# One unit of a decode-attention kernel loads half its keys and values in a row order that uses eight DMA engines

## The chip, the core and the metric

The kernel runs on one core of a Trainium2 chip. The metric is device time in microseconds (us) of one execution. All timed runs below are of the fast state (the one look named *alone* has no known state), and every ratio uses runs of the kernel before from the same chip and the same rounds. The kernel before takes 453.46 us (median; 453.44 to 454.08 in four runs).

Names: PE is the tensor engine, DVE and ACT the vector and scalar engines, SP the engine that issues the loads here. A *DMA engine* is one of the core's 16 transfer engines; it has nothing to do with PE, DVE and the rest. A *packet* is one record of the trace's DMA rows; here one row of keys or values for one SBUF partition, mostly 8 or 16 KB (4096 packets of 8 KB and 8064 of 16 KB in the load queue of the kernel before). A *landing* is one increment of a transfer's semaphore. A plain load has 16 landings in the trace, which I read as one for each DMA engine, and it is complete at the last one: PE started on unit 24's keys at 285.69 us, and their 16th landing was at 285.64 us.

## The reference

Two decode attentions with one query token each, concatenated. A sees all 8192 keys, B only the last 2048. There are 4 batches, 32 query heads, 8 key heads of width 128, all in bf16:

```python
q = (x @ wq)                         # 4 x 1 x 512 times 512 x 4096
scores = einsum("bhqd,bhkd->bhqk", q, k) * Dh ** -0.5   # k: cache, 8 heads, repeated 4 times
p = softmax(scores)
o = einsum("bhqk,bhkd->bhqd", p, v)
return o.reshape(B, 1, 4096) @ wo
```

There is little arithmetic per byte: 184.6 MB are read, mostly the two caches.

## The kernel before

The work is cut into 40 units: 8 of B (units 0 to 7), then 32 of A, one for each pair of key head and batch. A unit of A has 2 MB of keys and 2 MB of values. Partition p gets 64 consecutive keys (16 KB), so a load is 128 rows of 16 KB:

```python
NKS, NVS, NKT, NPT = 3, 4, 4, 3                # buffers for K, V, ...
def kv_src(cache, u, q=None):
    un = units[u]
    if un["P"] == 0:                           # attention A
        ap = cache[un["b"], un["g0"]].rearrange("(p t) d -> p t d", p=128)
        return ap if q is None else ap[:, q * TQ:(q + 1) * TQ, :]
    ...                                        # attention B: two halves
def sp_K(u):                                   # issue of a unit's keys, on SP
    waits = [("T", tjob_idx[(u - NKS, NB - 1)])] if u >= NKS else []
    ...
    op("sp", dma(kv_dst(K_sb, u % NKS, u), kv_src(KC[units[u]["P"]], u)), waits=waits, inc=("K", u))
```

PE transposes the keys (`L309` below), multiplies them with the queries (`L340`), and later multiplies the probabilities with the values (`L366`). It starts on a unit when the whole K load has landed. SP issues the K load of unit u when PE has transposed unit u-3, and the V load when PE has used the values of unit u-4. The order of keys within a unit does not matter to softmax, as long as K and V use the same one.

## Time and profile before

| | before |
|---|---|
| time, median | 453.46 us |
| share of the time in which the 16 DMA engines were busy with the load queue | 97.1% |
| rate in the middle of the run | 423 to 429 GB/s |
| PE busy | 83% |
| a 16 KB packet (trace, median of 274 to 294 us) | 613 ns |

The page of the kernel before: the span, the DMA rows in 40 slices, the queues, and the chain of waits that ended last.

```profile
span 452.2 us, 14586 instructions
...
DMA  8999999999999999999999999999999999999972
GB/s 346 401 414 418 451 402 418 419 417 428 408 416 430 424 423 424 428 426 424 428 425 425 428 423 429 423 425 423 425 426 426 427 425 423 430 420 428 423 332 80
DMA packets 17189, 185.51 MB, mean 410 GB/s; under 512 B 1748, under 2 KB 2280, under 8 KB 4712
...
q1 hardware_dynamic: 17048, 184.56, 97.1%
q8 instruction: 53, 0.87, 0.8%
...
DMA 60%; PE 33%; issue 3%; DVE 2%; ACT 1%; POOL 0%; POOLq 0%
```

Loads bound the kernel: the rate is flat near 425 GB/s from the first tenth to the end, and the chain is 60% DMA. PE's own lines (name, count, then busy us and ns of one, then the idle time before them and who ended it) show that it waits for keys and values:

```profile
L309 PE MATMUL ps<-identf,K_sb 128*128 128x128 f32 x1280 | 225.0, 337 | 37.7 <-DMA K_sb<-in_A_k_cache_dram 25.8
L366 PE MATMUL ps<-PT,V_sb 128*128 128x4 bf16 (+1 forms) x2560 | 76.6, 165 | 9.7 <-DMA V_sb<-in_A_v_cache_dram 7.5
```

The landings of the last load (last quarter of unit 39's values), read from the trace's semaphore records as us after the first one, show something that no share of busy time shows. It is not a view of the page, so it stands in an ordinary fence:

```
before   first 435.62 us: 0.0 0.2 0.4 0.8 0.8 1.8 2.3 4.7 | 9.3 9.4 9.4 9.7 10.7 10.8 10.9 11.0   last 446.62 us
```

Eight engines are done some 9 us (on average) before the other eight. The late ones lost their time in steps of some 1.5 us, near the packets of the instruction queue (q8 above: 53 packets of 16 KB and about 1.07 us each). That these packets are what makes the eight late is a reading of the trace.

### The profile page before, as it was taken

The page shows a single profiled execution, that of the slowest core. Times are in us where ns is not written, and L with a number is a line of the kernel's source. Part 1 is how long each engine was busy: PE and PEld are TensorE (multiplying, and loading weights), DVE is VectorE, ACT ScalarE, POOL GpSimd, SP SyncE. Part 2 cuts the span into 40 slices and gives each one's busy share as a digit, 9 for nine tenths or more (in the row PEclk, how much of TensorE's full clock was granted, in tenths as well). Part 3 has the DMA queues.
Part 4 walks back from the last instruction along what each step waited for, and adds up shares of the span by engine and source line. Part 5 has one row for each costly group of instructions (what it writes and reads, how often), then busy time and mean ns, then how long its engine had stood idle before and what let it go on. Part 6 is the DMA issues. An engine that isn't in the chain of part 4 may idle for free.

```text
span 452.2 us, 14586 instructions
## 1 busy us (share of the span) xinstructions
PE 374.6 (83%) x6781; PEld 344.9 (76%) x6781; DVE 196.4 (43%) x451; ACT 178.1 (39%) x202; POOL 35.6 (8%) x93
## 2 busy tenths in 40 slices
PE   0682379999859998989978898878989899888996
PEld 0682279987858797989768888867979799788895
DVE  0351225745634453434434543444445435434362
ACT  1150214524433362534334453434444434434261
POOL 1100000100100110000100010001000000000010
PEclk9996655859887985968878896969768858888596
DMA  8999999999999999999999999999999999999972
GB/s 346 401 414 418 451 402 418 419 417 428 408 416 430 424 423 424 428 426 424 428 425 425 428 423 429 423 425 423 425 426 426 427 425 423 430 420 428 423 332 80
DMA packets 17189, 185.51 MB, mean 410 GB/s; under 512 B 1748, under 2 KB 2280, under 8 KB 4712
## 3 DMA queue, kind: packets, MB, share of 16 engines
q1 hardware_dynamic: 17048, 184.56, 97.1%
q8 instruction: 53, 0.87, 0.8%
q14 instruction: 8, 0.07, 0.0%
q10 hardware_dynamic: 16, 0.01, 0.0%
q0 software_dynamic: 64, 0.01, 0.0%
HBM read 184.56 MB, written 0.01 MB: 408 GB/s over the span
## 4 chain that ended last, share of the span: by engine, by line
DMA 60%; PE 33%; issue 3%; DVE 2%; ACT 1%; POOL 0%; POOLq 0%
DMA K_sb<-in_A_k_cache_dram 30%; DMA V_sb<-in_A_v_cache_dram 24%; PE ps L309 18%; DMA W<-in_A_wq_dram 6%; PE ps L366 6%; PE ps L340 4%; PE ps L452 2%; PE ps L255 2%; DVE KT_sb L317 1%; ACT KT_sb L318 1%; DVE M L470 1%; PE ps L442 0%; DVE Dt L508 0%; PE ps L406 0%; DVE xo_sb L567 0%
## 5 line engine op out<-in xcount | busy, mean ns | idle before, releaser
L318 ACT ACTIVATE KT_sb<-ps 128x1024 bf16<-128x1024 bf16 x160 | 163.5, 1022 | 250.4 <-PE ps L309 250.2
L309 PE MATMUL ps<-identf,K_sb 128*128 128x128 f32 x1280 | 225.0, 337 | 37.7 <-DMA K_sb<-in_A_k_cache_dram 25.8
L309 PEld LDWEIGHTS ps<-identf,K_sb 128*128 128x128 f32 x1280 | 184.4, 174 | 50.8 <-DMA K_sb<-in_A_k_cache_dram 28.9
L317 DVE COPY KT_sb<-ps 128x512 int32<-128x512 int32 x160 | 110.4, 690 | 148.6 <-PE ps L309 147.9
L366 PE MATMUL ps<-PT,V_sb 128*128 128x4 bf16 (+1 forms) x2560 | 76.6, 165 | 9.7 <-DMA V_sb<-in_A_v_cache_dram 7.5
L366 PEld LDWEIGHTS ps<-PT,V_sb 128*128 128x128 bf16 x2560 | 71.0, 97 | 10.7 <-DMA V_sb<-in_A_v_cache_dram 8.3
L340 PEld LDWEIGHTS ps<-RQA,KT_sb 128*128 128x128 bf16 x2048 | 71.6, 99 | 3.6 <-issue 0.6
L340 PE MATMUL ps<-RQA,KT_sb 128*128 128x8 bf16 x2048 | 72.6, 167 | 0.9 <-ACT KT_sb L318 0.4
L540 POOL PARTITION_ALL_REDUCE LB<-L x40 | 17.3, 432 | 154.9 <-DVE L L531 154.9
L479 POOL PARTITION_ALL_REDUCE MB<-M x32 | 11.9, 371 | 176.9 <-DVE M L470 176.9
L470 DVE TENSOR_REDUCE M<-ps 128x4 f32<-128x256 f32 (+1 forms) x40 | 19.1, 477 | 12.7 <-PE ps L340 12.7
L557 DVE TENSOR_TENSOR OTg<-ps,RL 128x4 bf16<-128x4 f32 (+1 forms) x40 | 6.9, 174 | 40.2 <-PE ps L366 40.2
L531 DVE TENSOR_REDUCE L<-PT 128x4 f32<-128x256 bf16 (+1 forms) x40 | 21.9, 546 | 2.6 <-ACT PT L519 2.1
L340 PEld LDWEIGHTS ps<-RQB,KT_sb 128*128 128x128 bf16 x512 | 18.7, 102 | 2.6 <-issue 0.9
L340 PE MATMUL ps<-RQB,KT_sb 128*128 128x16 bf16 x512 | 19.0, 173 | 1.4 <-issue 0.9
L519 ACT ACTIVATE PT<-Dt 128x256 bf16<-128x256 f32 (+1 forms) x40 | 18.1, 452 | 3.3 <-DVE Dt L508 3.2
L452 PE MATMUL ps<-W,OL 128*4 128x512 bf16 x60 | 17.1, 432 | 0.0
L255 PE MATMUL ps<-xT,W 128*128 128x4 bf16 x256 | 7.5, 166 | 11.0 <-DMA W<-in_A_wq_dram 10.6
L255 PEld LDWEIGHTS ps<-xT,W 128*128 128x128 bf16 x256 | 7.2, 104 | 11.1 <-DMA W<-in_A_wq_dram 10.7
L508 DVE TENSOR_TENSOR Dt<-ps,MB 128x256 f32<-128x256 f32 x32 | 13.3, 415 | 0.5 <-POOL MB L479 0.5
L234 PE MATMUL ps<-ident,xo_sb 4*128 4x4 bf16 x8 | 0.6, 170 | 14.2 <-POOL identf L581 14.2
L414 DVE CAST OL<-ps 32x16 bf16<-32x16 f32 (+1 forms) x36 | 6.5, 182 | 11.1 <-PE ps L406 10.7
(43 smaller groups left out, 53.5 us busy)
## 6 DMA issues: line engine op xcount, KB each, us to landing
K_sb<-in_A_k_cache_dram SPq DMA_DIRECT2D x32, 2048.0 KB, 22.1
V_sb<-in_A_v_cache_dram SPq DMA_DIRECT2D x31, 2048.0 KB, 27.0
K_sb<-in_B_k_cache_dram SPq DMA_DIRECT2D x16, 1024.0 KB, 18.7
V_sb<-in_B_v_cache_dram SPq DMA_DIRECT2D x16, 1024.0 KB, 21.8
W<-in_B_wq_dram SPq DMA_DIRECT2D x1, 4096.0 KB, 12.6
W<-in_B_wo_dram SPq DMA_DIRECT2D x1, 4096.0 KB, 34.3
W<-in_A_wq_dram SPq DMA_DIRECT2D x1, 4096.0 KB, 29.2
W<-in_A_wo_dram SPq DMA_DIRECT2D x1, 3584.0 KB, 30.1
```

What stands on the lines that cost most here:

```text
L255: ins = pe.matmul(out=bk[:, hl * Bn:(hl + 1) * Bn], lhsT=W1wq[:, c, hq * DH:(hq + 1) * DH], rhs=xT[:, P, c, :], start=(c == 0), stop=(c == ...
L309: ins = pe.transpose(out=bkf[:, pi * 128:(pi + 1) * 128], in_=K_sbf[:, slot, t0:t0 + 2, :].rearrange("p t d -> p (t d)"), identity=identf[ ...
L317: return e.tensor_copy(out=KT_sb.bitcast(I32)[:, tj % NKT, :], in_=bkf.bitcast(I32)[:, :])
L318: return e.activation(out=KT_sb[:, tj % NKT, :], in_=bk[:, :], func=ACTF.Copy)
L340: ins = pe.matmul(out=stb[:, t * CPT:(t + 2) * CPT], lhsT=ktv[:, pi, :, e], rhs=rhs, start=(e == 0), stop=(e == 1))
L366: ins = pe.matmul(out=otb[:, s * CPT:(s + 1) * CPT], lhsT=V_sb[:, vs, t, :], rhs=pt_cols(u, t * CPT, CPT), start=(j == 0), stop=(j == J - 1))
L452: ins = pe.matmul(out=opb[0:Bn, 0:D], lhsT=lhsT, rhs=wo_view[:, hq0 // REP + i // REP, i % REP, :], start=(first and i == 0), stop=(last a ...
L470: return dve.tensor_reduce(out=M1[:, 0:NC].rearrange("p (s h) -> p s h", h=CPT), in_=stb[:, 0:NT * CPT].rearrange("p (s j h) -> p s h j", ...
L508: return dve.tensor_tensor(out=Dt[:, 0:NT * CPT].rearrange("p (s j h) -> p s j h", s=S, h=CPT), in0=stb[:, 0:NT * CPT].rearrange("p (s j h ...
L519: return act.activation(out=PT[:, u % NPT, 0:NW], in_=Dt[:, 0:NW], func=ACTF.Exp, scale=scale)
L531: return dve.tensor_reduce(out=L1[:, 0:NC].rearrange("p (s h) -> p s h", h=CPT), in_=PT[:, u % NPT, 0:NT * CPT].rearrange("p (s j h) -> p ...
L540: return pool.partition_all_reduce(LB[:, 0:NC], L1[:, 0:NC], channels=128, reduce_op=ReduceOp.add)
```

## The change

The intent: unit 24, in the middle of A, is loaded in two halves of 32 keys per partition. The first half uses the row order 8 x 16 instead of 128 in a row. The two narrow loads, with a slowest dimension of 8 on the source side, I read as running on eight DMA engines. The second half is plain. K and V get the same order, so the result stands.

```diff
+    NARROW = NU_B + (NU - NU_B) // 2          # unit 24
     def kv_src(cache, u, q=None):
         un = units[u]
+        if u == NARROW:
+            half = SK // 2
+            RB = (half // 128) * DH
+            base = cache[un["b"], un["g0"], q * half:(q + 1) * half, :]
+            return bass.AP(tensor=base.tensor, offset=base.offset,
+                           ap=[[RB, 8], [8 * RB, 16], [1, RB]] if q == 0 else [[RB, 128], [1, RB]])
...
         def sp_K(u):
             waits = ...
-            if units[u]["P"] == 1:
-                op("sp", dma(kv_dst(K_sb, u % NKS, u, 0), kv_src(KC[1], u, 0)), waits=waits, inc=("Kh", u))
-                op("sp", dma(kv_dst(K_sb, u % NKS, u, 1), kv_src(KC[1], u, 1)), inc=("K", u))
+            if units[u]["P"] == 1 or u == NARROW:
+                kc = KC[units[u]["P"]]
+                op("sp", dma(kv_dst(K_sb, u % NKS, u, 0), kv_src(kc, u, 0)), waits=waits, inc=("Kh", u))
+                op("sp", dma(kv_dst(K_sb, u % NKS, u, 1), kv_src(kc, u, 1)), inc=("K", u))
                 return
...                                            # sp_V and kv_dst likewise
```

More of the change, by code (lines that the diff above doesn't have):

```diff
@@ L83, in kv_dst @@
         un = units[u]
-        if un["P"] == 1:
+        if un["P"] == 1 or u == NARROW:
             JB = NT // 2
@@ L760, in sp_V @@
                        waits=waits if q == 0 else [], inc=("VL", q))
-            elif units[u]["P"] == 1:
-                op("sp", dma(kv_dst(V_sb, u % NVS, u, 0), kv_src(VC[1], u, 0)), waits=waits, inc=("Vh", u))
-                op("sp", dma(kv_dst(V_sb, u % NVS, u, 1), kv_src(VC[1], u, 1)), inc=("V", u))
+            elif units[u]["P"] == 1 or u == NARROW:
+                vc = VC[units[u]["P"]]
+                op("sp", dma(kv_dst(V_sb, u % NVS, u, 0), kv_src(vc, u, 0)), waits=waits, inc=("Vh", u))
+                op("sp", dma(kv_dst(V_sb, u % NVS, u, 1), kv_src(vc, u, 1)), inc=("V", u))
             else:
```

## The prediction

> **What bounds the kernel.** DMA. The page shows DMA 97% busy on the one data queue, 410 GB/s, 185.5 MB; PE is 83% busy and waits for K and V (the chain of waits: 60% DMA, K 30%, V 24%). In the packet records a 16 KB packet takes 611 to 621 ns[...]: about 26.7 GB/s for each of 16 engines. Transfers are issued 22 (K) to 27 us (V) before they land, about five 2 MB transfers ahead, so no engine runs dry.
>
> **The engines do not finish together.** Each transfer's semaphore has 16 landings in the trace[...]. They spread over 0.7 us at first, 6.6 us by unit 24, 11.0 us for the last transfer (first engine 435.6, last 446.6 us). At the end there are two groups of eight: 0 to 4.8 us and 9.3 to 11.0 us. The late ones lose about 1.5 us at a time, roughly when one of the 53 16 KB packets of the instruction queue (about 1.07 us each) passes. [...] The 4-row store of B's output, queued behind a V load, landed at four times matching that load's offsets 0.6, 1.0, 1.4 and 2.7 us[...].
>
> **What the change does.** Unit 24's first K half and first V half (1 MB each) have a slowest source dimension of 8[...]. Early engines get 64 KB more per transfer, late ones 64 KB less: 64 KB is 8 packets of 8 KB at about 312 ns, 2.5 us. For K and V together +5.0 us[...]. Two extra issues (0.6 us each on SP) are hidden by SP's waits. PE, DVE and ACT work is unchanged; K and V share one row permutation, so the result stands.
>
> **Critical path.** A transfer is complete when its slowest engine lands. At the end: late group 9.3..11.0 minus 5.0 gives 4.3..6.0; early group 0..4.8 plus 5.0 gives 5.0..9.8. The last landing moves from 11.0 to about 9.8: 1.2 us earlier (445.4). Just after unit 24 the spread is 1 us worse (2.8 + 5.0 against 6.6), which only delays PE where it has slack. The tail (PV of the last unit, 1.5 us of PE stall at 445) can take about that gain.
>
> **Risk.** [...]if packets there double to about 620 ns, those four lose up to 10 us more, and the end is up to 4.7 us later (458). I give this a third.
>
> **Prediction.** 452.6 us, 8 in 10 within 451.3 to 457.5. Faster by over 2%: 0.02; within 2%: 0.95; slower by over 2%: 0.03.
>
> **What would show it.** Landings of the two narrow halves: 8 late ones[...]; K24 complete later by 1 us or less, then a last-transfer spread of 5 to 6 us instead of 11; last landing about 445.4. Wrong if: 8 KB packets near unit 24 take 600 ns;[...] or the tail is held by PE's own issue (453.4).

The sum of the forecast: early engines 0 to 4.8 + 5.0 = 5.0 to 9.8 us, late ones 9.3 to 11.0 - 5.0 = 4.3 to 6.0 us, so the last landing moves from 11.0 to 9.8 us, 1.2 us earlier. That all eight engines which get the additional bytes are early, and that the risk is one of four engines, are in it as my estimates, not shown by the trace. What the trace shows is that the four landings of the store came 0.4, 0.8 and 2.1 us apart from the first, as four of the first eight landings of that V load did. Of a 16 KB packet it shows 611 to 624 ns from the 1st to the 99th percentile of 8064 packets, but 47 took over 900 ns.

## The result

The changed kernel takes 476.43 us (475.02 to 477.1, four runs). The ratio is 1.050, with a 95% interval of 1.047 to 1.053: slower by 23 us, outside the range and with the wrong sign. (A ratio here is the mean time of one kernel's runs over that of the other's of the same rounds, so it is not quite the ratio of the medians.)

The page of the changed kernel, the same lines:

```profile
span 475.3 us, 14588 instructions
...
DMA  8999999999999999999999999999999999999970
GB/s 354 394 412 430 421 419 419 419 419 419 410 430 422 430 420 429 423 428 422 425 426 426 427 236 273 303 241 401 418 426 426 427 421 427 423 427 392 421 299 28
DMA packets 17461, 185.51 MB, mean 390 GB/s; under 512 B 1764, under 2 KB 2296, under 8 KB 4728
...
q1 hardware_dynamic: 17320, 184.56, 96.5%
...
DMA 82%; PE 14%; SPq 1%; ACT 1%; DVE 1%; issue 0%
...
L317 PE MATMUL ps<-identf,K_sb 128*128 128x128 f32 x1280 | 221.8, 333 | 58.6 <-DMA K_sb<-in_A_k_cache_dram 44.8
...
L374 PE MATMUL ps<-PT,V_sb 128*128 128x4 bf16 (+1 forms) x2560 | 76.4, 165 | 18.5 <-DMA V_sb<-in_A_v_cache_dram 17.7
```

The DMA row still says 9 (90% or more) in all but the first and the last two slices, so the engines were hardly idle, but in four slices of 11.9 us the rate is 236, 273, 303 and 241 GB/s. The time was lost there. PE does the same work (222 us against 225 us in the transposes; their line is L317 now) and waits 19 us more for keys and 10 us more for values.

Cut by windows, first before, then after. The columns are the window and its length, then busy us of PE, PEld (weight loads), DVE, ACT and POOL, then PE's granted clock, the busy share of the DMA engines, and GB/s:

```profile
254.00:274.00 20.00, 17.93 (x359) 15.99 (x356) 9.65 (x24) 9.05 (x11) 1.60 (x4) 0.91 1.01 427
274.00:294.00 20.00, 16.61 (x332) 16.02 (x329) 8.29 (x19) 8.69 (x10) 1.60 (x4) 0.84 1.00 424
294.00:300.00 6.00, 3.37 (x17) 2.60 (x15) 2.17 (x5) 1.30 (x2) 0.37 (x1) 0.51 0.99 415
300.00:320.00 20.00, 18.35 (x342) 16.97 (x341) 9.73 (x24) 8.76 (x12) 1.60 (x4) 0.84 1.01 426
```

```profile
254.00:274.00 20.00, 18.39 (x350) 16.44 (x347) 9.56 (x23) 9.05 (x11) 1.61 (x4) 0.83 1.01 425
274.00:294.00 20.00, 10.56 (x181) 10.15 (x177) 4.70 (x11) 4.40 (x5) 1.18 (x3) 0.61 1.02 234
294.00:300.00 6.00, 2.38 (x11) 2.38 (x12) 1.02 (x2) 0.38 (x1) 0.00 (x0) 0.50 0.96 396
300.00:320.00 20.00, 13.52 (x208) 12.33 (x206) 6.58 (x14) 7.01 (x9) 1.24 (x3) 0.69 1.01 247
```

Two stretches of 20 us, one for K and one for V of unit 24, run at 234 and 247 GB/s with fully busy engines. Against 424 and 426 GB/s that is 20 x (1 - 234/424) + 20 x (1 - 247/426) = 9.0 + 8.4 = 17.4 us of lost transfer, three quarters of the 23 us. The chain of waits of the changed kernel in this stretch (start, length, what) is two waits for values. The longest wait for values in the chain before was 27.6 us:

```profile
265.62 37.81 DMA V_sb<-in_A_v_cache_dram
...
305.78 39.18 DMA V_sb<-in_A_v_cache_dram
```

The packet records say what "busy at half the rate" is. In 274 to 294 us (ordinary fence, counted from the trace's packet records):

```
before   16 KB: 514 packets, median  613 ns,   3 over 900 ns     8 KB: none
after    16 KB: 165 packets, median 1129 ns, 165 over 900 ns     8 KB: 237 packets, median 586 ns, 235 over 450 ns
```

Nearly every packet took nearly double: also the plain 16 KB rows of other loads. All 16 engines were busy (DMA share 1.02), so this includes the eight that have no part in the narrow load. That is neither what I predicted (8 KB packets at 312 ns and two halves of the engines shifted by 5 us) nor quite what I named as the risk (four engines slowed, up to 10 us).

### The profile page after: what moved, and what is told of

Read it like the earlier page. It is cut to its first block, busy times and chain, and to the rows that moved or that the text cites. A ratio compares the mean times of both kernels' runs of the same rounds, so it can differ in the third digit from the quotient of the medians.

```text
span 475.3 us, 14588 instructions
## 1 busy us (share of the span) xinstructions
PE 370.0 (78%) x6781; PEld 340.5 (72%) x6781; DVE 195.9 (41%) x451; ACT 178.4 (38%) x202; POOL 35.8 (8%) x93
## 4 chain that ended last, share of the span: by engine, by line
DMA 82%; PE 14%; SPq 1%; ACT 1%; DVE 1%; issue 0%
DMA V_sb<-in_A_v_cache_dram 45%; DMA K_sb<-in_A_k_cache_dram 24%; PE ps L317 9%; DMA K_sb<-in_B_k_cache_dram 7%; DMA W<-in_A_wq_dram 6%; PE ps L374 3%; PE ps L348 2%; SPq L620 1%; ACT KT_sb L326 1%; PE ps L450 0%; PE ps L263 0%; PE ps L414 0%; DVE Dt L516 0%; DVE M L478 0%; PE ps L392 0%
## 5 line engine op out<-in xcount | busy, mean ns | idle before, releaser
L317 PE MATMUL ps<-identf,K_sb 128*128 128x128 f32 x1280 | 221.8, 333 | 58.6 <-DMA K_sb<-in_A_k_cache_dram 44.8
L317 PEld LDWEIGHTS ps<-identf,K_sb 128*128 128x128 f32 x1280 | 181.0, 172 | 72.9 <-DMA K_sb<-in_A_k_cache_dram 48.4
L548 POOL PARTITION_ALL_REDUCE LB<-L x40 | 17.4, 434 | 173.1 <-DVE L L539 173.1
L487 POOL PARTITION_ALL_REDUCE MB<-M x32 | 11.9, 373 | 188.1 <-DVE M L478 188.1
L460 PE MATMUL ps<-W,OL 128*4 128x512 bf16 x60 | 16.1, 411 | 0.0
L263 PE MATMUL ps<-xT,W 128*128 128x4 bf16 x256 | 7.4, 165 | 10.9 <-DMA W<-in_A_wq_dram 10.6
L263 PEld LDWEIGHTS ps<-xT,W 128*128 128x128 bf16 x256 | 7.0, 101 | 11.1 <-DMA W<-in_A_wq_dram 10.7
L422 DVE CAST OL<-ps 32x16 bf16<-32x16 f32 (+1 forms) x36 | 6.5, 182 | 16.5 <-PE ps L414 16.2
## 6 DMA issues: line engine op xcount, KB each, us to landing
K_sb<-in_B_k_cache_dram SPq DMA_DIRECT2D x16, 1024.0 KB, 21.4
```

What stands on the lines that cost most here:

```text
L263: ins = pe.matmul(out=bk[:, hl * Bn:(hl + 1) * Bn], lhsT=W1wq[:, c, hq * DH:(hq + 1) * DH], rhs=xT[:, P, c, :], start=(c == 0), stop=(c == ...
L317: ins = pe.transpose(out=bkf[:, pi * 128:(pi + 1) * 128], in_=K_sbf[:, slot, t0:t0 + 2, :].rearrange("p t d -> p (t d)"), identity=identf[ ...
L460: ins = pe.matmul(out=opb[0:Bn, 0:D], lhsT=lhsT, rhs=wo_view[:, hq0 // REP + i // REP, i % REP, :], start=(first and i == 0), stop=(last a ...
L548: return pool.partition_all_reduce(LB[:, 0:NC], L1[:, 0:NC], channels=128, reduce_op=ReduceOp.add)
```

## The experiments

Three theories to begin with. **Destination**: it matters which SBUF partitions the narrow loads write. (The expectations call this the *port theory*, and a run is named after it; the name is a guess at a mechanism, and no run shows one.) **Source**: the interleaved rows are slow to read from memory. **Engines**: a load on only eight engines is slow by itself. In the edits, `W2` is the weight buffer of attention B, whose contents are no longer needed by unit 24; it serves as a spare destination.

### Same eight engines, other destinations: own_ports

```diff
-  one load: 128 partitions, source [[RB, 8], [8 * RB, 16], [1, RB]]
+  four loads of 32 partitions, source [[RB, 8], [8 * RB, 4], [1, RB]], to
+  K_sb[0:32], K_sb[32:64], W2[0:32], W2[32:64]     (V likewise)
```

> Unit 24's first K half and V half stay on eight engines and keep the interleaved row order, but as four loads of 32 partitions each, all to partitions 0-63 (two of the four to a spare buffer; the result is wrong on purpose). Port theory[...]: 8 KB packets stay near 313 ns, no slow phase, 452 to 454 us. Source theory (the interleaved rows are slow to read): slow packets stay, 470 us or more. Engine theory (a transfer on eight engines is slow by itself): 470 us or more.

Measured: 457.61 us, ratio 1.009 (1.007 to 1.011). The result is wrong. Windows of this run:

```profile
274.00:294.00 20.00, 15.94 (x317) 15.56 (x314) 8.20 (x18) 8.45 (x11) 1.60 (x4) 0.83 1.00 421
294.00:300.00 6.00, 5.09 (x114) 4.56 (x110) 2.63 (x6) 2.53 (x3) 0.37 (x1) 0.97 1.03 426
300.00:320.00 20.00, 18.06 (x318) 15.94 (x316) 7.99 (x21) 7.78 (x10) 1.23 (x3) 0.75 1.00 419
```

The slow phases are gone: 421 and 419 GB/s, 8 KB packets at a median of 313 ns. Same number of engines and bytes, nearly the same row order; what differs is the partitions written, and the cut into four loads, which quadrants and upper_only below share without being fast. So nearly 19 us of the 23 (476.4 - 457.6) come from *where* the eight engines write. But the kernel is still 4 us slower than before, not 1 us faster, so a second step of the prediction is wrong as well. The landings of the last load show which:

```
before      first 435.62 us: 0.0 0.2 0.4 0.8 0.8 1.8 2.3 4.7 9.3 9.4 9.4 9.7 10.7 10.8 10.9 11.0   last 446.62 us
own_ports   first 439.46 us: 0.0 0.2 0.7 0.7 1.0 1.0 1.4 2.2 2.2 2.2 2.3 3.0 3.7 6.3 | 10.4 10.9   last 450.32 us
```

Had all eight narrow engines been early ones, the last landing could not be later than about 435.6 + 4.7 + 5.0 = 445.3 us. It is at 450.3 us, and two engines stand apart from the other 14. I read this as two of the eight engines that carry the narrow loads being of the late group: they were charged the 5 us instead of relieved of it. The landings of a load soon after unit 24 show the split itself (us before the last landing, which is at 324.91 us):

```
own_ports   16.2 16.2 | 10.2 10.2 10.0 8.7 8.7 8.5 | 6.4 5.6 5.6 4.8 4.8 2.4 | 0.4 0.0
```

By that reading these are two early engines that were relieved, six late ones that were relieved, six early ones that were charged and two late ones that were charged: six and two where the prediction had eight and none. The lead of the first two shrinks to 10.9 us by the end.

### Same destinations, other rows: blocks_of_16

```diff
-  [[RB, 8], [8 * RB, 16], [1, RB]]
+  [[32 * RB, 8], [RB, 16], [1, RB]]       # groups of 16 consecutive rows
```

> As the changed kernel[...], written to the same partitions. Source theory: slow phase gone, about 453 us. Port theory and engine theory: unchanged, 475 to 477 us, with two phases of about 20 us in which every packet takes double.

Measured: 476.37 us, ratio 1.050 (the result is wrong), and 240 and 247 GB/s in the two windows:

```profile
274.00:294.00 20.00, 10.14 (x186) 9.79 (x183) 4.69 (x11) 4.49 (x6) 1.17 (x3) 0.67 1.01 240
...
300.00:320.00 20.00, 13.52 (x208) 12.38 (x206) 6.57 (x14) 7.49 (x9) 1.23 (x3) 0.64 1.01 247
```

The time and the two slow phases are the same, so the order of reading is not the cause; the source theory falls.

### The same kind of order on 16 engines: sixteen

```diff
-  [[RB, 8], [8 * RB, 16], [1, RB]]
+  [[RB, 16], [16 * RB, 8], [1, RB]]
```

> As the changed kernel, but the row order is 16 x 8 instead of 8 x 16, so the two loads run on all 16 engines (the result stays right). Engine theory: 453 to 454 us. Source theory: still slow packets, 465 us or more. [...]

For the destination theory the expectation left the result open.

Measured: 467.29 us, ratio 1.031 (1.029 to 1.032), correct. From 274 to 289 us, 110 of 118 packets of 16 KB were over 900 ns, at 239 GB/s. The load is on all 16 engines here (16 landings each), and it is slow all the same: the engine theory falls. Which partitions each engine wrote, no record shows.

### One of the two loads: k_only

```diff
 V of unit 24:
-  first half [[RB, 8], [8 * RB, 16], [1, RB]]
+  first half [[RB, 128], [1, RB]]
```

> The change for the K half alone; V of unit 24 in two plain halves. Every theory: one slow phase of about 20 us instead of two, so half the loss, 463 to 466 us. If it is more than two thirds or less than a third of the 23 us, the two transfers do not simply add.

Measured: 463.32 us, ratio 1.022 (1.020 to 1.024): 10 us of 23, one slow phase (249 GB/s from 274 to 294 us, 422 GB/s from 300 to 320 us). That is near the half which the expectation gave for two loads that add.

### Partitions of all quarters, and of the upper half alone: quadrants and upper_only

```diff
-  K_sb[0:32], K_sb[32:64], W2[0:32],   W2[32:64]          # own_ports
+  K_sb[0:32], K_sb[32:64], K_sb[64:96], K_sb[96:128]      # quadrants: result correct
+  K_sb[64:96], K_sb[96:128], W2[64:96], W2[96:128]        # upper_only
```

> Correct result, all 128 partitions, eight engines, as four loads of 32 partitions[...]. Port theory with plain sharing (estimate: a small queue model with 611 ns per 16 KB packet[...]):[...] +9.7 us, about 463 us, and packets of both lengths in each phase. [...]

> As own_ports, but to partitions 64-127 only (wrong result on purpose)[...]. Port theory, same queue model: +14.6 us, 468 us, nearly all packets doubled while it lasts. If partitions play no part: as own_ports, 457.6 us.

The 463 and 468 us are my estimates: besides the measured 611 ns the queue model took as given which engines would meet, and no record shows that. For a slowdown that goes beyond equal sharing in pairs I had put 468 to 476 us for quadrants.

Measured: quadrants 470.78 us (1.037, correct), upper_only 479.08 us (1.056). In upper_only, from 274 to 292 us, all 119 packets of 16 KB were over 900 ns (median 1234) and all 230 of 8 KB over 450 ns (median 631), at 213 GB/s. The window of upper_only to set beside that of own_ports (421 GB/s):

```profile
274.00:294.00 20.00, 11.27 (x178) 10.82 (x175) 4.69 (x11) 4.40 (x5) 1.18 (x3) 0.59 1.01 219
```

Between own_ports and upper_only only the destination partitions differ, 0-63 against 64-127, and that is worth 21 us. Both runs are slower than the queue model with fair sharing in pairs gave (463 and 468 us).

### The lower half again, in two loads: low_blocks

```diff
-  four loads of 32 partitions (0-63), source [[RB, 8], [8 * RB, 4], [1, RB]]
+  two loads of 64 partitions (0-63), source [[RB, 8], [8 * RB, 8], [1, RB]]
```

> As own_ports (partitions 0-63 only, wrong result on purpose), but as two loads of 64 partitions[...]. Queue model: +21.5 us[...], about 475 us, with 16 KB packets of the eight other engines left at 611 ns. [...]

Measured: 473.73 us, ratio 1.045. The time agrees with the model (about 475 us), but by chance, since the packets do not: from 274 to 290 us 88 of 138 packets of 16 KB were over 900 ns, while the model leaves those of the eight other engines at 611 ns. Eight engines at that rate would have moved 3.4 MB in these 16 us (an estimate: 8 x 16384 B / 611 ns x 16 us); the packets that were not slow, of 16 and of 8 KB, moved 1.4 MB. So the slowdown reaches engines other than the eight. Against own_ports (457.61 us) the destination is the same set of partitions; what changed is how the rows are cut into loads, 8 x 8 twice against 8 x 4 four times.

### The balance by itself: four_engines

This tests the other half of the prediction, on partitions of the half that was fast in own_ports (421 GB/s), and with a slowest dimension of 4, like the store of B's output, whose four landings had matched early ones. By my estimate the four engines get 96 KB more (12 packets of 8 KB at 313 ns, 3.7 us) and the others 32 KB less (1.2 us).

```diff
-  K, first half: [[RB, 8], [8 * RB, 16], [1, RB]]      (V likewise)
+  K, 16 keys per partition plainly, 512 KB; and 512 KB as four loads of 16 partitions,
+  source [[RB, 4], [4 * RB, 4], [1, RB]], to W2[0:16], W2[32:48]   (V: plain halves)
```

> Tests the balancing idea[...]: half of unit 24's first K half goes plainly, 512 KB go on four engines to partitions 0-15 and 32-47 of a spare buffer (wrong result on purpose); V plain. [...] If the four are early and the last transfer's slowest engine sets the end: 452.0 to 452.6 us (1.2 us faster). If one of them is in the late group: about 457 us. If the balance does not matter: 453.4 us.

Measured: 452.34 us, ratio 0.9972 (0.9959 to 0.9984, five rounds). That is 1.1 us faster than before, as the sum said, and the last landing is at 445.45 us instead of 446.62 us. So the sum "a load's slowest engine ends the kernel, and bytes moved off an engine take their packets' time off it" (here 32 KB less on twelve engines, 1.2 us) holds when the right engines are chosen. This is not a usable kernel: half of that K half goes to a spare buffer and stale keys are used (the comparison with the reference still passes).

### Four engines, then two, to the upper half: four_upper and two_upper

```diff
 four_engines:
-  W2[0:16], W2[32:48]
+  W2[64:80], W2[96:112]                                          # four_upper
+  W2[64:72], W2[96:104], source [[RB, 2], [2 * RB, 4], [1, RB]]  # two_upper: 256 KB; the other 256 KB plainly
```

> Identical to four_engines but for the destination: partitions 64-79 and 96-111 of the spare buffer instead of 0-15 and 32-47[...]. Plain sharing, pairs only: while it lasts (10 us) at most 4 of the 12 other engines show doubled 16 KB packets, and the time is about 457 us. [...] If the destination plays no part: 452.3 us.

> Only two engines write partitions[...] (64-71 and 96-103), 16 rows of 8 KB each; the other bytes of the half go plainly. Pairs only: 2 of 14 other engines doubled, so about one in seven 16 KB packets over 0.9 us during 10 us; rate in that stretch about 370 GB/s; 453 to 458 us. If the slowdown spreads: most 16 KB packets over 0.9 us and a rate near 230 to 300 GB/s; 457 us or more.

For four_upper, if the slowdown spreads, I had put most 16 KB packets over 0.9 us and 459 us or more. That two_upper's narrow loads run on two engines is taken from the pattern of the landings: 4 for the store with a slowest dimension of 4, 8 for 8, 16 for 16.

Measured: 458.02 us (1.0096) and 458.11 us (1.0091). Windows of four_engines, of four_upper and of two_upper:

```profile
276.00:286.00 10.00, 8.35 (x161) 8.19 (x160) 4.10 (x9) 4.38 (x5) 0.80 (x2) 0.84 1.02 425
```

```profile
276.00:286.00 10.00, 7.09 (x92) 6.92 (x92) 2.81 (x6) 3.38 (x4) 0.43 (x1) 0.67 1.03 230
```

```profile
276.00:286.00 10.00, 6.68 (x132) 6.40 (x130) 3.42 (x9) 3.69 (x5) 0.80 (x2) 0.83 1.02 232
```

And the packets from 277 to 286 us:

```
four_engines   16 KB: 135 packets, median  613 ns,  2 over 900 ns     8 KB: 157, median 313 ns,  0 over 450 ns
four_upper     16 KB:  57 packets, median 1232 ns, 57 over 900 ns     8 KB:  83, median 622 ns, 83 over 450 ns
two_upper      16 KB:  55 packets, median 1247 ns, 52 over 900 ns     8 KB:  66, median 640 ns, 61 over 450 ns
```

This is the clearest pair. Moving the destination of four_engines by 64 partitions costs 6 us and doubles every packet. With only *two* engines on the narrow loads, a slowdown confined to pairs would reach one packet in seven (two of the other 14 engines, an estimate); 52 of 55 were slow. Two such engines are enough to bring the whole core's loads down to 55% (232 GB/s against 425). My model of fair pairs falls here, by the packets and the rates; the time of four_upper, 458.0 us, lies between its two forecasts (about 457, and 459 or more) and decides nothing. Why the slowdown spreads, no view shows.

### The split alone: halves_plain

```diff
-  [[RB, 8], [8 * RB, 16], [1, RB]] if q == 0 else [[RB, 128], [1, RB]]
+  [[RB, 128], [1, RB]]
```

> Control: unit 24's K and V in two halves of 8 KB rows, plain order, all 16 engines. Every theory: 453.3 to 454.0 us, 8 KB packets near 313 ns. If it is over 455 us, the split itself costs.

Measured: 453.92 us, ratio 1.0006 (0.9991 to 1.002). Two more loads and rows of 8 KB cost nothing that these runs can tell.

### With nothing else under way: alone

```diff
+  before all other loads, each waited for before the next, all to W2:
+  (1) slowest dimension 8, partitions 0-63   (2) slowest dimension 2, partitions 64-71 and 96-103
+  (3) the changed load: slowest dimension 8, all 128 partitions
```

> The plain-halves kernel with three extra loads before all others, each waited for before the next, so that no other load is under way: (1) 8 engines to partitions 0-63[...]; (2) 2 engines to partitions 64-71 and 96-103; (3) the changed load[...]. [...] If only other traffic makes it slow: all three near 312 ns. The total time (about 475 us) says nothing here.

Two of the three cases were: (1) and (2) near 312 ns and (3) near 600 ns, if the engines of (3) slow one another; (2) and (3) near 600 ns, if writing such partitions as those of (2) is slow by itself.

One look (one execution, so its state is not known; only its packets are used). In (1), 56 of 64 packets of 8 KB took 309 ns; the 8 slow ones are the eight that started first. In (2), 28 of 32 took 309 ns. In (3), from 16.5 to 25 us, the median was 596 ns, 99 of 116 packets were over 450 ns, and the rate was 112 GB/s (all 128 packets: median 612 ns, 111 over 450 ns). So the destination of (2) is not slow by itself. The changed load is slow even without other traffic, which agrees with the first of the cut cases: eight engines at 8192 B / 309 ns each would have moved 212 GB/s (an estimate), and it moved 112. By what mechanism, no view shows.

## Why the prediction was wrong

- **Right**: DMA bounds the kernel; the engines end up to 11 us apart in two groups of eight; eight engines carry the narrow load and the other eight pass it by (each narrow load has 8 landings besides the increment at its issue); the last load's slowest engine sets the end, and moving bytes between the groups moves the end by the computed amount (four_engines: 1.1 us, computed 1.2). That the prediction's own gain was also 1.2 us is a coincidence: four_engines moves other amounts.
- **Wrong, and the larger part**, the step called Risk: "if packets there double to about 620 ns, those four lose up to 10 us more, and the end is up to 4.7 us later". The central forecast counted 8 KB packets at 312 ns, and the risk let only four engines double. Measured were 586 ns, and not on four engines but on all 16, for some 20 us for each of the two loads (165 of 165 packets of 16 KB over 900 ns in 274 to 294 us, 161 of 189 in 300 to 320 us). Unit 24's keys were complete at 297.6 us instead of 285.6 us by the landings, 12 us later, where the prediction said 1 us or less. The doubling cost 17.4 us by the rates, and nearly 19 us by the difference of the changed kernel and own_ports. I had treated the slowdown as a matter of a few engines; two_upper shows that loads on two engines are enough to slow nearly every packet (52 of 55). I had also taken it for a risk of one in three, and had not asked whether the changed load is slow by itself, as it is with nothing else under way (alone, part 3: 111 of 128 packets over 450 ns).
- **Wrong, and smaller**, the choice of the engines. The store had four landings that matched early ones, and I extended that to all eight engines of the narrow loads. By the landings, two of the eight that carried the narrow loads are late. In own_ports they turn the predicted gain of 1 us into a loss of 4 us. It was an extrapolation from four engines, and the test of it was not in the trace of before.
- If the two simply add, 17.4 us of slow transfer and 4 us for the two late engines make 21.4 of the 23 us. The changed kernel has the same two stragglers: in its last load 14 engines landed within 4.7 us, two at 10.1 and 11.1 us. The rest is not assigned.
- Of the checks that the prediction named, the one that decided was listed under "Wrong if": 8 KB packets near unit 24 at 600 ns.

What stays open: by what mechanism the narrow loads slow the packets of other engines; and which partitions each engine got, since no record names them. What is shown is that the destination partitions decide (own_ports 457.61 us against upper_only 479.08 us), and that the way the rows are cut into loads matters too (low_blocks, 473.73 us to the same partitions as own_ports). No usable kernel faster than the one before came out: the load that helped, four_engines, writes 32 partitions of a spare buffer, and quadrants, which puts all 128 partitions right by such loads, costs 3.7%.

## What to carry to other kernels

In these runs the row order of a load went with its number of landings (4, 8 and 16 for slowest dimensions of 4, 8 and 16), and with some destinations such loads brought the rate of the whole core down to nearly half (213 to 249 GB/s against 419 to 427) while every DMA engine looked fully busy (a share of 1.01 to 1.03 in the windows above). So look at the GB/s row, not at the busy row, and at the time of a packet: 16 KB in 613 ns was healthy here, 1.1 us was not. And before shifting load to "the idle engines", find out for each of them that it is idle.
